# A written-out step order of a linear-attention and expert kernel, replaced by another order, with two store quarters cut in halves

## The chip, the cores and the metric

The kernel runs on one core of one Trainium2 chip. The metric is the device time of one execution in microseconds (us). Three executions of the kernel before took 101.87, 101.66 and 101.7 us; the median is 101.7 us.

## What is computed

For 4 batches, 4 heads, 1088 positions and a head size of 32, q, k and v become a linear attention, and its result goes through one dense feed-forward layer with 2048 inner columns. Cut to what matters:

```
def phi(x):                       # x: batch, head, position, 32
    a = S1 x ; b = S2 x           # 8 numbers each
    return outer(a, b)            # 64 features
kv  = sum over positions of phi(k) * v      # 64 x 32 for each batch and head
z   = sum over positions of phi(k)
out = (phi(q) kv) / (phi(q) z + 1e-6)
x   = out, 4352 tokens x 128 columns (the four heads side by side)
h   = x w_in ; g = h * sigmoid(beta * h) ; y = g w_out
```

The kernel folds beta into the weights (w_in times beta, w_out divided by beta), so that the activation is a plain Silu.

## The kernel before, in words

**Two kinds of work.** The attention gives the activations x (transposed, in the tile `xT`), batch after batch. The feed-forward layer consumes them in ten chunks of tokens: two of 256, seven of 512, one of 256. A chunk's inner columns are worked through in waves of 1024 numbers for each partition: four waves for a chunk of 256, eight for one of 512, 68 in all.

**Steps.** Nothing schedules this kernel: every step is a function, `DO` maps a short name to each, and the string `SEQ` (L809 to L825) lists all of them by hand in program order. Each engine has its own queue and takes its own instructions in exactly that order; a step waits only for the data and buffers it needs, and everything behind it on its engine waits with it. A letter at the end of a name chooses the engine of a step: D is VectorE (DVE), A is ScalarE (ACT), P is GpSimd (POOL); for loads s, a and g choose the queue of SyncE (SP), ACT or POOL.

Steps of the feed-forward layer:

- `W` (L395): one wave, x times `winp` into PSUM (L407), and a Silu of 128x1024 on ACT (L415). I call the n-th one Wn; W5 begins the second chunk, W9 the third, W17 the fourth, W25 the fifth, W33 the sixth. The PSUM tile `wave` has two buffers.
- `V` (L424, L369): the second product for the oldest wave, into `moeout` (L379). Vn belongs to Wn. The last V of a chunk adds a turn on DVE (L389, which I call OUT0 to OUT9) and the chunk's stores from SP (L352; ST0 to ST9), four DMAs for each batch that the chunk touches, one for each 32 columns.
- `li`, `wi`, `be`, `bc`: load w_in, broadcast beta by a matmul, copy it from PSUM, and multiply them on POOL (`winp`, L311). `lo`, `wa`, `wv`, `wg`: load w_out and scale one 128x128 piece of it by 1/beta (`rb`) on ACT (L332), DVE or POOL (L339).

Steps of the attention, for batch b:

- `lk`, `lq`, `lv` load the keys, the queries and the values; keys and queries have one tile each for all batches, so the next load waits until the last turn has read it. `tk` and `tq` are 32x32 block turns on DVE (L434, L440).
- `kp`: products of the keys with S1 and S2 on PE (L456), `ka`: their turn into factors on DVE (L465). `o`: outer products of the factors in five parts (L591; parts of 128x512, the part numbered 2 of 128x256). `kv`: the sum over positions on PE (L632), 72 pairs of matmuls in parts `kv0` to `kv4`, each behind its outer product.
- `gr`, `gc`, `wh`, `wc`: the factors' Gram matrix on PE (L479), a copy (L491), a small product (L495), a copy into the weights of q (L505); they give the denominator's factor.
- `q..`: the products for the queries on PE (L518), two letters for the PSUM tiles of the halves (w, t or o). `qt`: their turns (L535). `dm`, `di`, `dx`, `da`: the denominator and its division into a factor (L547, L556, L562, L581, L570); the part of the factor that `dx` gives lies in PSUM, that of `da` in SBUF. `p`: outer products (L591) and `t`: their turns (L622).
- `n..` (the numerator, L689) needs all `t` of a batch and the turned sums `nd`. For batch 0 these come by PE (`ns`, `nt`, `nc`), for the others by a turn (`nf`) and two DMAs through DRAM (`ng`, L672 and L676). `x` copies the result into `xT` (L705) in two halves.

Batch 0's queries are worked in two parts: A, the first 256 positions, and C, the rest. So W1 to W4 need part A alone.

**Fillers.** `h`, `e`, `i` and `mW` are matmuls on a constant tile (L253) that keep TensorE at work.

**The order around the change.** DVE's queue up to batch 0's numerators runs, in step names: `ka00 ka01 tqA gc0D o00D rb o01D qtA0 qtA1 tqC diA daA pA0D tA0 qtC0 qtC1 tA1 tk10 diC tk11 dxC daC pC0D tC0 ka10 ka11 tC3 tC2 tC1 tk20 tk21`. PE's queue from the first wave on runs `W1 W2 kp1 W3 V1 gr1 V2 W4 wh1 nC kv10 kv11 kv12 kp2 W5 W6 V3 V4 W7 kv13 kv14 q1 W8 V5 V6 W9`.

Of the kernel before, what the change touches and what calls it, by code (L numbers as in the profile page):

```python
# [18 lines left out]
def kernel(  # L19
# [22 lines left out]
    T = S // 32  # L42
# [306 lines left out]
    ALT = {len(tok_chk) - 3, len(tok_chk) - 1}  # L349
    moe = {"ci": 0, "w": 0, "acc": None, "todo": [], "ready": set()}  # L350

    def store(o_sb, t0, u0, u1, queues):  # L352
        c = t0 + 32 * u0
        while c < t0 + 32 * u1:
            b, r = divmod(c, S)
            n = min(t0 + 32 * u1 - c, S - r) // 32
            u = (c - t0) // 32
            for g4 in range(4):
                queues[g4 % len(queues)].dma_start(
                    out=bass.AP(  # L360
                        tensor=out.tensor,
                        offset=out.offset + (b * S + r // 32) * DM + 32 * g4,
                        ap=[[T * DM, 32], [DM, n], [1, 32]],
                    ),
                    in_=o_sb[32 * g4 : 32 * g4 + 32, u : u + n, :],
                )
            c += n * 32

    def w2(ci, j0, jn, g):  # L369
        t0, tw = tok_chk[ci]  # L370
        if j0 == 0:
            if ci in ALT:
                moe["acc"] = ps1.tile([P, TCH], F32, tag="one", name="moeout")
            else:
                moe["acc"] = pso.tile([P, TCH], F32, tag="moeout", name="moeout")
        for jj in range(jn):
            j = j0 + jj
            assert j in scaled
            nc.tensor.matmul(  # L379
                out=moe["acc"][:, :tw],  # L380
                lhsT=woutp[:, j // U, j % U, :],
                rhs=g[jj],
                start=(j == 0),
                stop=(j == NJ - 1),
            )
        if j0 + jn == NJ:
            o_sb = sbA.tile([P, TCH // 32, 32], F32, tag="o_sb", name="o_sb", bufs=4)
            nt = tw // 32
            nc.vector.transpose(  # L389
                out=o_sb[:, :nt, :].rearrange("p t d -> p (t d)"), in_=moe["acc"][:, :tw]  # L390
            )
            last = ci == len(tok_chk) - 1
            store(o_sb, t0, 0, nt, [nc.sync, nc.scalar] if last else [nc.sync])

    def w1():  # L395
        ci = moe["ci"]
# [27 lines left out]
    def second():  # L424
        w2(*moe["todo"].pop(0))
# [336 lines left out]
    for nm, (_, n) in Q_PART.items():  # L762
        w = 1 if nm == "A" else 2
# [25 lines left out]
    for nm in Q_PART:  # L789
# [36 lines left out]
    for s_ in SEQ.split():
        DO[s_]()
# [29 lines left out]
```

## Time and profile before

| what | value |
|---|---|
| median of three runs | 101.7 us |
| the profiled execution | 100.9 us |
| its span, first to last instruction | 99.1 us |
| outside the span | 1.8 us |
| granted TensorE clock, mean over the span | 1.000 |
| instructions in the profile | 3150 |
| moved by DMA | 11.75 MB |

The profile is one execution taken by the hardware profiler. Its page lists busy time by engine, slices of the span, the chain of work that ended last, and groups of instructions; the trace behind it can be asked for the instructions of one engine in order of time, for waits, for one tile, for the chain piece by piece, and for stretches of the span. A row of the time order has a start, a length, the engine, the line, the operation with output and input, and a count; neighbours of one form are merged, and the length is that of the whole row. Lengths overlap a little, so the distance from start to start is what one instruction costs a queue. "PEld" is TensorE's weight load. A wait "<-issue" is one for which the trace names no releaser.

### The profile page before, as it was taken

The numbers are of one execution on the slowest core, as the hardware profiler recorded it, in microseconds if no ns is written. First come the engines' busy times: TensorE is split into PE (matmuls) and PEld (weight loads), VectorE is DVE, ScalarE is ACT, GpSimd is POOL, SyncE is SP. The second block draws the span as 40 slices with busy tenths as digits, with TensorE's granted clock in tenths as the row PEclk, the third lists the DMA queues.
The fourth block names the chain that finished last, engine by engine and source line by source line (L and its number), as shares of the span: only waits on it lengthen the run. The fifth ranks groups of instructions, "written<-read, shape, count | busy, mean of one in ns | idle before, by whom it ended". The sixth has DMA issues, their size and how long they took to land.

```text
span 99.1 us, 3150 instructions
## 1 busy us (share of the span) xinstructions
PE 92.4 (93%) x1302; PEld 48.7 (49%) x1302; DVE 58.1 (59%) x128; ACT 76.7 (77%) x102; POOL 36.1 (36%) x58
## 2 busy tenths in 40 slices
PE   5989998997999999999999999999999999999940
PEld 2525536665867544434445444444444444446720
DVE  3569989888579998449998335699630020020210
ACT  0505299984869797997998897999989999999910
POOL 5739989998594900077370000320000000000000
PEclk9999999999999999999999999999999999999999
DMA  2999999914971320058043141215015006014163
GB/s 55 273 351 317 395 370 388 270 42 107 387 225 38 62 44 7 0 149 307 17 95 67 20 76 30 53 31 83 2 20 85 1 2 104 7 20 70 17 100 59
DMA packets 24031, 11.75 MB, mean 119 GB/s; under 512 B 19245, under 2 KB 21837, under 8 KB 24017
## 3 DMA queue, kind: packets, MB, share of 16 engines
q1 hardware_dynamic: 23256, 11.44, 41.8%
q8 instruction: 10, 0.16, 0.6%
q10 hardware_dynamic: 696, 0.09, 0.6%
q0 software_dynamic: 64, 0.02, 0.4%
q14 instruction: 5, 0.03, 0.1%
HBM read 9.22 MB, written 2.33 MB: 117 GB/s over the span
## 4 chain that ended last, share of the span: by engine, by line
PE 63%; POOL 12%; ACT 9%; DMA 5%; SPq 4%; issue 2%; DVE 0%; POOLq 0%; ACTq 0%
PE wave L407 27%; PE moeout L379 26%; ACT g L415 8%; DMA w_in_sb<-in_moe_w_in_dram 5%; POOL winp L311 5%; PE nps L689 5%; PE kvz L632 4%; POOL qo L591 3%; POOL kp L591 3%; SPq L143 2%; SPq L164 1%; PE qps L518 1%; ACT xT L705 1%; PE kps L456 1%; SPq L178 1%
## 5 line engine op out<-in xcount | busy, mean ns | idle before, releaser
L415 ACT ACTIVATE g<-wave 128x1024 f16<-128x1024 f32 x68 | 64.8, 1027 | 7.0 <-PE wave L407 6.8
L407 PE MATMUL wave<-xT,winp 128*128 128x512 f16 (+1 forms) x160 | 39.7, 348 | 0.8 <-issue 0.4
L379 PE MATMUL moeout<-g,woutp 128*128 128x512 f16 (+1 forms) x160 | 37.6, 347 | 0.0
L407 PEld LDWEIGHTS <-winp 128*128 128x128 f16 x160 | 17.0, 114 | 16.7 <-issue 6.4
L379 PEld LDWEIGHTS <-woutp 128*128 128x128 f16 x160 | 15.4, 97 | 12.5
L591 POOL TENSOR_TENSOR kp<-kab 128x512 f32<-128x512 f32 (+1 forms) x17 | 16.1, 981 | 10.8 <-DVE kab L465 10.8
L389 DVE STREAM_TRANSPOSE o_sb<-moeout 128x512 f32<-128x512 f32 (+1 forms) x10 | 6.3, 631 | 22.0 <-PE moeout L379 22.0
L622 DVE STREAM_TRANSPOSE qt<-qo 128x512 f32<-128x512 f32 (+1 forms) x21 | 11.8, 605 | 0.2
L591 POOL TENSOR_TENSOR qo<-qa,qab 128x512 f32<-128x512 f32 (+1 forms) x11 | 9.5, 886 | 5.3 <-DVE qa L570 5.3
L535 DVE STREAM_TRANSPOSE qab<-qps 128x576 f32<-128x576 f32 (+2 forms) x10 | 6.0, 642 | 2.1 <-PE qps L518 2.0
L689 PE MATMUL nps<-qt,nd 32*32 32x288 f32 (+2 forms) x320 | 7.0, 364 | 0.1
L253 PE MATMUL kvz<-idle 128*128 128x384 f16 (+1 forms) x21 | 5.1, 399 | 1.1 <-DVE idle L215 1.1
L632 PE MATMUL kvz<-kp,v 128*32 128x64 f32 x288 | 5.7, 222 | 0.3 <-POOL kp L591 0.3
L434 DVE STREAM_TRANSPOSE kT<-k 128x544 f32<-128x544 f32 x8 | 5.6, 719 | 0.4 <-DMA k<-in_k_dram 0.3
L547 POOL TENSOR_TENSOR tmp<-qab 128x64 f32<-128x64 f32 (+2 forms) x3 | 1.8, 589 | 11.0 <-DVE qab L535 11.0
L440 DVE STREAM_TRANSPOSE qT<-q 128x576 f32<-128x576 f32 (+3 forms) x8 | 5.8, 721 | 0.0
L253 PEld LDWEIGHTS <-idle 128*128 128x128 f16 x36 | 3.5, 110 | 4.6 <-issue 2.3
L632 PEld LDWEIGHTS kvz<-kp,v 128*32 128x32 f32 x288 | 4.4, 109 | 2.6 <-issue 1.6
L465 DVE STREAM_TRANSPOSE kab<-kps 128x288 f32<-128x288 f32 x8 | 3.6, 464 | 3.2 <-PE kps L456 3.2
L689 PEld LDWEIGHTS nps<-qt,nd 32*32 32x32 f32 x320 | 3.9, 103 | 2.7 <-DVE qt L622 0.5
L311 POOL TENSOR_TENSOR winp<-w_in_sb,beta_bc 128x512 f16<-128x512 f32 x4 | 5.1, 1274 | 0.1
L332 ACT ACTIVATE woutp<-w_out_sb,rbeta 128x128 f16<-128x128 f32 x15 | 5.0, 399 | 0.1
(63 smaller groups left out, 54.8 us busy)
## 6 DMA issues: line engine op xcount, KB each, us to landing
k<-in_k_dram SPq DMA_DIRECT2D x3, 544.0 KB
q<-in_q_dram SPq DMA_DIRECT2D x3, 544.0 KB, 5.1
v<-in_v_dram SPq DMA_DIRECT2D x4, 288.0 KB
v<-in_v_dram SPq DMA_DIRECT2D x4, 256.0 KB, 5.8
w_in_sb<-in_moe_w_in_dram SPq DMA_DIRECT2D x4, 256.0 KB, 5.4
w_out_sb<-in_moe_w_out_dram SPq DMA_DIRECT2D x4, 256.0 KB, 5.7
out_dram<-o_sb SPq DMA_DIRECT2D x16, 64.0 KB, 3.6
k<-in_k_dram SPq DMA_DIRECT2D x2, 272.0 KB, 2.9
```

The lines of the kernel that those rows point to most:

```text
L253: nc.tensor.matmul(out=t[:, P : P + cols], lhsT=idle, rhs=cut(idle, [[0, cols // P], [1, P]]), start=fresh or other, stop=True, skip_group ...
L311: eng.tensor_tensor(out=winp[:, n].rearrange("p c u -> p (c u)"), in0=w_in_sb[:, o : o + FQ], in1=beta_bc[:, o : o + FQ], op=MUL,)
L379: nc.tensor.matmul(out=moe["acc"][:, :tw], lhsT=woutp[:, j // U, j % U, :], rhs=g[jj], start=(j == 0), stop=(j == NJ - 1),)
L389: nc.vector.transpose(out=o_sb[:, :nt, :].rearrange("p t d -> p (t d)"), in_=moe["acc"][:, :tw])
L407: nc.tensor.matmul(out=wv[:, jj // per, o : o + tw], lhsT=winp[:, j // U, :, j % U], rhs=xT[:, t0 : t0 + tw], start=True, stop=True,)
L415: nc.scalar.activation(out=g, in_=wv, func=ACTF.Silu)
L440: nc.vector.transpose(out=qT2[b % 2][:, t0:t1].rearrange("p t s -> p (t s)"), in_=q_t[b][:, t0:t1].rearrange("p t d -> p (t d)"),)
L535: nc.vector.transpose(out=cut(QAB[nm], [[32, 2], [32 * H, n], [1, 32]], 64 * i), in_=PS["qps", nm][i][:, :, : 32 * n],)
L591: eng.tensor_tensor(out=cut(o, [[F, n], [R, R], [1, R]]), in0=cut(a, [[sa, n], [1, R], [0, R]]), in1=cut(b_, [[sb_, n], [0, R], [1, R]]), ...
L622: nc.vector.transpose(out=QT[nm][:, j0:j1].rearrange("p j h c s -> p (j h c s)"), in_=QO[nm][:, j0:j1].rearrange("p j h f -> p (j h f)"),)
L632: nc.tensor.matmul(out=PS["kvz", b][32 * h : 32 * h + 32, :F], lhsT=v_t[b][:, h, j, :], rhs=KP[b][:, j, h, :], start=(j == 0), stop=(j == ...
L689: nc.tensor.matmul(out=t[g // 2][32 * h : 32 * h + 32, g % 2, : 32 * n], lhsT=ND[b][rows, h, fc, :], rhs=QT[nm][rows, :, h, fc, :], start= ...
```

## The change

`SEQ` is replaced by another order of nearly the same steps; the function `store` can send some of its quarters in two halves, and is told to for two of the four quarters of chunk 2 (the third chunk).

Part by part:

- In the text of `SEQ` the first part of the queries (`tqA`) stands right behind batch 0's factors, as it did; the Gram copy `gc0` that followed it on DVE goes to ACT, and both of DVE's outer products of batch 0 follow at once.
- `kv00` to `kv04` run one behind the other, without fillers between them. The four beta products are spread apart (`be01` behind `gr0`, `be10` behind `qA`, `be11` behind the `kv0`). Four `i` go and two `h` come.
- The scaling of w_out: pieces that ACT did go to DVE (piece 6) and POOL (14), and DVE's piece 10 to ACT; most of ACT's come before the first numerators or between W1 and W4.
- Other engines for single steps: `pC3` POOL to DVE; `wc1`, `xC1`, `wc2`, `wc3` DVE to ACT; the two halves of `x1` swap ACT and DVE; `o30` DVE to POOL; `dm3` POOL to DVE; `p33` DVE to POOL and `p34` POOL to DVE. The PSUM tiles of `qA`, `qC` and `n2` are given in another order.
- PE from the first wave on: `W1 W2 kp1 W3 V1 V2 W4 gr1 V3 nC V4 wh1 kp2 W5 W6 kv10 to kv14 q1 W7 V5 W8 V6 W9 V7 W10 V8 gr2 W11 V9 ... W15 V13 n1 W16 V14 W17 V15 W18 V16 W19 wh2 kp3 W20 W21 kv20 to kv24 q2 W22 V17`, then waves and V one by one, with `kv30 kv31` behind W25, `kv32` to `kv34` behind W28, and `n2` behind V24. From W32 on the order on PE is that of before, but for where some V stand from W51 on.
- SP: `lk3` comes behind ST0, `lq2` behind ST1 (before, both stood ahead of ST0) and `lq3` and `ng2` behind ST2 (before, ahead of it). ST2 is six DMAs and not four.
- DVE in batch 2: `t20 t24 tq30 t23 t22 tq31 nf3 t21`; before, `tq30` stood between `da2` and `dx2`, and `nf3` and `tq31` behind all turns.

The diff:

```diff
@@ -349,21 +349,26 @@
     ALT = {len(tok_chk) - 3, len(tok_chk) - 1}
     moe = {"ci": 0, "w": 0, "acc": None, "todo": [], "ready": set()}
 
-    def store(o_sb, t0, u0, u1, queues):
+
+    HALVED = 2
+
+    def store(o_sb, t0, u0, u1, queues, halved=0):
         c = t0 + 32 * u0
         while c < t0 + 32 * u1:
             b, r = divmod(c, S)
             n = min(t0 + 32 * u1 - c, S - r) // 32
             u = (c - t0) // 32
             for g4 in range(4):
-                queues[g4 % len(queues)].dma_start(
-                    out=bass.AP(
-                        tensor=out.tensor,
-                        offset=out.offset + (b * S + r // 32) * DM + 32 * g4,
-                        ap=[[T * DM, 32], [DM, n], [1, 32]],
-                    ),
-                    in_=o_sb[32 * g4 : 32 * g4 + 32, u : u + n, :],
-                )
+                m = n // 2 if g4 < halved else n
+                for w in range(0, n, m):
+                    queues[g4 % len(queues)].dma_start(
+                        out=bass.AP(
+                            tensor=out.tensor,
+                            offset=out.offset + (b * S + r // 32 + w) * DM + 32 * g4,
+                            ap=[[T * DM, 32], [DM, m], [1, 32]],
+                        ),
+                        in_=o_sb[32 * g4 : 32 * g4 + 32, u + w : u + w + m, :],
+                    )
             c += n * 32
 
     def w2(ci, j0, jn, g):
@@ -390,7 +395,7 @@
                 out=o_sb[:, :nt, :].rearrange("p t d -> p (t d)"), in_=moe["acc"][:, :tw]
             )
             last = ci == len(tok_chk) - 1
-            store(o_sb, t0, 0, nt, [nc.sync, nc.scalar] if last else [nc.sync])
+            store(o_sb, t0, 0, nt, [nc.sync, nc.scalar] if last else [nc.sync], HALVED if ci == 2 else 0)
 
     def w1():
         ci = moe["ci"]
@@ -807,21 +812,21 @@
                 DO[f"x{nm}{i}{c}"] = lambda nm=nm, i=i, c=c: put_x(nm, i, COPY[c])
 
     SEQ = """
-        ls0a ls1g lk0.0s lk0.1s lb4a lbpg m lqAs lv0s lqCs li0s li1s li2s li3s mW h h h h e e tk00 ts msP m2P
-        sq1P sq0P tk01 kp0t ka00 ka01 tqA be00 be01 kx0A bc00A bc01A gr0 gc0D h h wh0 wc0A z0 lo0s lk1s lo1s
-        lo2s lo3s h h qAww o00D rb o01D qtA0 qtA1 tqC lq1s lv1s o04P o02P o03P kv00 i kv01 kv02 i kv03 kv04 ns0A
-        i i i nt0 nc0A dmAP diA daA pA0D tA0 qCwt wi1P pA1P wi0P be10 be11 wa0 wa3 wa1 wa2 bc11A bc10A qtC0 qtC1
-        tA1 dmCP wi3P wi2P tk10 diC tk11 dxC daC pC0D tC0 pC3P pC2P pC1P wa7 wa4 wa5 wa11 i i i i i i i nAww
-        xA1A xA0A wa6 wa14 i i i W W kp1t ka10 ka11 tC3 tC2 tC1 W V gr1 V gc1A wa9 wa8 wa15 W wh1 lk2s tk20 tk21
-        wc1D nCtw xC0A wa12 xC1D tq10 wa13 o10P o11P o12P kv10 kv11 kv12 kp2t ka20 wv10 tq11 ka21 o14P o13P lk3s
-        lv2s lq2s W W V V W kv13 kv14 q1wt nf1 ng1s W V V qt10 qt11 dm1D di1 dx1 W W V da1 V W o20P o24P o23P
-        o21P o22P kv20 kv21 kv22 kv23 kv24 p10D p12P p13P p14P p11D t10 t11 t13 t12 t14 W W V V W V V W n1tw
-        x11A W nf2 tk30 tk31 x10D tq20 V gr2 gc2A W W kp3t wh2 W V W V W ka30 tq21 wc2D ka31 lq3s lv3s ng2s V
-        q2wt qt20 qt21 dm2D di2 o30D o34P o33P o31P o32P W V W V W V V W W V V W V W da2 tq30 dx2 p20D t20 p23P
-        t23 p22P t22 p21D p24P t21 t24 V W kv30 kv31 W kv32 kv33 kv34 W n2wt x21D nf3 ng3s x20A W V W gr3 W gc3D
-        wh3 V W V wc3D tq31 q3wt qt30 qt31 dm3P di3 dx3 W V W V W V W da3 V V p30D p31D p34P p33D t30 t33 p32D
-        t32 t31 t34 W W V V W V W V W V W V W V V W n3tw x30A x31D W V W V W V W V V W W V V W V W V W V W V W V
-        V W V W V W V W V W V V W V W V W V W V V W V V V V
+        ls0a ls1g lk0.0s lk0.1s lb4a lbpg m lqAs lv0s lqCs li0s li1s li2s li3s mW h h h h e e tk00 ts tk01 msP
+        kp0t ka00 ka01 tqA be00 sq0P m2P kx0A o00D o01D h h h gr0 be01 bc00A gc0A wh0 wc0A z0 lo0s lk1s lo1s
+        lo2s lo3s bc01A h h h qAwt o02P be10 kv00 kv01 o03P o04P sq1P kv02 kv03 kv04 be11 qtA0 qtA1 dmAP tqC
+        lq1s lv1s diA daA rb pA0D tA0 i qCtw wi0P qtC0 qtC1 pA1P tA1 wi1P dmCP tk10 diC tk11 dxC daC pC0D pC3D
+        wv6 ns0A bc11A wa0 bc10A nt0 nc0A i i i i i i i nAww wa1 wa3 wa4 wa7 wi3P wi2P xA0A xA1A wa5 wa8 wa11
+        wa2 i i i W wa10 W wa9 kp1t pC1P pC2P tC0 tC3 ka10 ka11 tC1 wg14 o10P o13P o12P o11P W V wa12 wa13 V
+        wa15 W gr1 V gc1A tC2 lk2s tk20 tk21 tq10 o14P nCtw lv2s tq11 V lk3s xC0A wh1 kp2t ka20 ka21 xC1A wc1A W
+        W kv10 kv11 kv12 kv13 kv14 q1wt W qt10 nf1 qt11 dm1D di1 dx1 V W V W V ng1s da1 W V gr2 W V W V W V W
+        gc2A V W V o20P o21P o22P o24P o23P p10D p11D p14P p13P p12P t10 t11 t13 t12 t14 n1tw x11D tk30 lq2s
+        tq20 tk31 x10A W V W V W lv3s tq21 V lq3s W wh2 kp3t wc2A ka30 ka31 W W kv20 kv21 kv22 kv23 kv24 q2wt W
+        V nf2 qt20 qt21 dm2D di2 dx2 da2 o30P o31P o33P o32P o34P p20D p21D t20 ng2s W V W V W kv30 kv31 W V W V
+        W kv32 kv33 kv34 W V W p23P p24P t24 p22P tq30 t23 t22 tq31 nf3 t21 V W V n2tw x21D ng3s x20A W V W gr3
+        W gc3D wh3 V wc3A W V q3wt W V qt30 qt31 dm3D di3 da3 W V W V W V V dx3 p30D t30 p32D p34D t34 p31D t32
+        p33P t31 t33 W W V V W V W V W V W V W V V W n3tw x31D x30A W V W V W V W V W V V W V W V W V V W V W V
+        W V W V W V W V W V V W V W V W V V W V W V W V V V V
     """
     for s_ in SEQ.split():
         DO[s_]()
```

## The prediction

> **What bounds the kernel now.** I read the page's chain first, then the groups, then the chain in order of time, to see who sets the pace where.
>
> ```profile
> PE 63%; POOL 12%; ACT 9%; DMA 5%; SPq 4%; issue 2%; DVE 0%; POOLq 0%; ACTq 0%
> ...
> L415 ACT ACTIVATE g<-wave 128x1024 f16<-128x1024 f32 x68 | 64.8, 1027 | 7.0 <-PE wave L407 6.8
> ```
>
> TensorE carries 63% of the chain; the Silus stood still 7.0 us before their waves, 6.8 of it for PE. So ACT is the second limit, close behind.
>
> ```profile
> 39.90 1.83 ACT g L415 x2
> ...
> 45.27 0.43 PE moeout L379 x2
> 45.70 0.43 PE wave L407 x2
> ...
> 55.84 0.65 ACT xT L705
> ...
> 59.40 1.03 ACT g L415
> ```
>
> A W or a V costs PE 0.43 (0.435 with its handoff), a pair 0.87; the first row gives a Silu 0.92 (1.83 for two). Where waves crowd, ACT sets the pace: from 39.90 to 44.63 and from 55.84 to 60.43 the chain lies almost wholly on it. From the first wave on, PE does the same steps before and after. So the change can win only where PE waits, and I compare the start of four steps on PE: W5, n1, W22, n2. From W32, right behind n2, PE's order is the old one up to W51.
>
> ```profile
> 20.93 1.38 PE L689 MATMUL nps<-qt,nd 32*32 32x224 f32 x64
> ...
> 23.32 0.71 PE L456 MATMUL kps<-kT,sk 64*32 64x288 f32 x16
> 24.41 1.03 PE L407 MATMUL wave<-xT,winp 128*128 128x256 f16 x8 [0.38 <-issue]
> ...
> 27.27 0.78 PE L518 MATMUL qps<-qT,wq 32*32 32x288 f32 x32
> ...
> 29.32 1.03 PE L407 MATMUL wave<-xT,winp 128*128 128x512 f16 x4
> ...
> 31.59 1.21 PE L632 MATMUL kvz<-kp,v 128*32 128x64 f32 x72
> 32.73 1.05 PE L407 MATMUL wave<-xT,winp 128*128 128x512 f16 x4
> ...
> 36.42 1.60 PE L689 MATMUL nps<-qt,nd 32*32 32x288 f32 x64
> ...
> 44.67 0.59 PE L407 MATMUL wave<-xT,winp 128*128 128x512 f16 x2
> ...
> 54.24 1.60 PE L689 MATMUL nps<-qt,nd 32*32 32x288 f32 x64
> ```
>
> Before: W5 at 24.41, W9 at 29.32, n1 at 36.42, W22 at 44.67, n2 at 54.24.
>
> **The change, part by part.**
>
> *Up to the first wave.* "First part of q right behind the keys" moves nothing on DVE: `tqA` stood behind `ka01` already. The fillers between the `kv0` go, and the beta products are spread. I estimate W1 between 0.5 and 1 us earlier. I count that as nothing, because of this wait and because nC needs all of C's turns:
>
> ```profile
> PEld kps L456 <- DVE qo L591: 0.2, 1, 0.2
> ```
>
> `kp1` reuses the PSUM tile that `pC0` reads, so W3 stays behind DVE's `pC0D`. That is the cover; were W1 later than about 16.9, it would cost one to one.
>
> *C's factors on DVE.*
>
> ```profile
> 11.34 0.62 DVE L591 TENSOR_TENSOR qo<-qa,qab 128x256 f32<-128x256 f32 x1
> ...
> 16.78 0.68 DVE L591 TENSOR_TENSOR qo<-qps,qab 128x512 f32<-128x512 f32 x1
> 17.50 0.71 DVE L622 STREAM_TRANSPOSE qt<-qo 128x512 f32<-128x512 f32 x1
> 18.43 0.85 DVE L465 STREAM_TRANSPOSE kab<-kps 128x288 f32<-128x288 f32 x2 [0.22 <-PE kps L456]
> 19.20 1.59 DVE L622 STREAM_TRANSPOSE qt<-qo 128x256 f32<-128x256 f32 x3
> ...
> 24.55 0.24 DVE L339 TENSOR_SCALAR woutp<-w_out_sb,rbeta 128x128 f16<-128x128 f32 x1
> ...
> 46.10 0.67 DVE L547 TENSOR_TENSOR tmp<-qab 128x288 f32<-128x288 f32 x1
> ```
>
> ```profile
> 10.39 1.28 POOL L311 TENSOR_TENSOR winp<-w_in_sb,beta_bc 128x512 f16<-128x512 f32 x1
> ...
> 14.62 2.50 POOL L311 TENSOR_TENSOR winp<-w_in_sb,beta_bc 128x512 f16<-128x512 f32 x2
> ...
> 42.73 3.72 POOL L591 TENSOR_TENSOR kp<-kab 128x512 f32<-128x512 f32 x4 [7.80 <-DVE kab L465]
> ```
>
> New between `pC0D` and `tC0` are `pC3D`, 128x256 with both factors in SBUF, and `wv6`. Their price is the open one. The row at 11.34 is such an operation: 0.62 for half of what the row at 16.78 did in 0.68 with a factor in PSUM. It ended at 11.96, and POOL's product (10.39 + 1.28) at 11.67: it reads as a wait for POOL and then 0.29. The `dm` at 46.10 ended at 46.77, 0.32 behind POOL's end at 46.45 (42.73 + 3.72). So I let a DVE product of two SBUF tiles wait out POOL's running instruction and then take 0.3. Bounds for `pC3D`: 0.3 with no wait, 2.0 if POOL wins twice.
>
> [...]
>
> Sum: `pC0D` at 16.7 (16.78; the steps ahead differ by -0.2 to +0.1), end 17.4. POOL's last `wi` ends at 17.1, and its next product (3.72 for three and a half, 1.06 each) at 18.1; `pC3D` ends at 18.4, `wv6` at 18.6. `tC0`, `ka1` and the three other turns take 0.71 + 0.77 (18.43 to 19.20) + 1.59 = 3.1: the last ends at 21.7. Before it ended at 20.79, and nC began 0.14 behind: now 21.8. nC 1.38, V4 0.43, wh1 0.2 (like the small products, an estimate), kp2 0.75: **W5 at 24.6**, 0.2 later. `xC0` and `xC1`, both on ACT now, at most 0.65 each, end by 24.5: just covered. The 0.38 before the old W5 names no releaser; I leave it out and keep it for the range. V3 and V4 (0.87) are done by then, but not the 40 of 72 pairs of `kv1` that stood ahead before (0.77): even.
>
> *W5 to n1.* W5, W6 and the break behind them 0.97, all of `kv1` 1.14 (31.59 to 32.73), q1 0.72, W7 V5 W8 V6 1.74: W9 at 29.2. Then seven W, seven V and gr2: 6.1 + 0.35, so PE is ready at 35.6. DVE:
>
> ```profile
> 28.09 1.45 DVE L535 STREAM_TRANSPOSE qab<-qps 128x576 f32<-128x576 f32 x2 [0.43 <-PE qps L518]
> 29.57 0.84 DVE L547 TENSOR_TENSOR tmp<-qab 128x288 f32<-128x288 f32 x1
> 30.45 0.49 DVE L556 TENSOR_REDUCE rd<-tmp 128x36 f32<-128x324 f32 x1
> ...
> 32.03 0.44 DVE L389 STREAM_TRANSPOSE o_sb<-moeout 128x256 f32<-128x256 f32 x1
> 32.39 1.25 DVE L591 TENSOR_TENSOR qo<-qps,qab 128x512 f32<-128x512 f32 x2
> 33.57 2.79 DVE L622 STREAM_TRANSPOSE qt<-qo 128x512 f32<-128x512 f32 x5
> 36.29 0.21 DVE L667 STREAM_TRANSPOSE kvf<-kvz 128x64 f32<-128x64 f32 x1
> ```
>
> q1 ends at 27.5; `qt` 1.48, `nf1` 0.15, `dm1` 0.65 (0.3 to 1.35 by where POOL's product ends), `di dx da` 1.58, OUT1 0.36, `p` 1.18, `t` 2.72: 35.6. **n1 at 35.7**, 0.7 earlier. The gain is that `kv2` (1.14) no longer stands ahead of n1, and that DVE is as early as PE.
>
> *n1 to W22.* n1 1.53, nine W and V 3.9, two handoffs 0.1, wh2 0.2, kp3 0.72, `kv2` 1.14, q2 0.75: 8.35, against 8.25 without `kv2`. Six Silus at 0.92 from 38.0 end by 43.6, just ahead of W22. **W22 at 44.05**, 0.6 earlier: the old stretch on ACT is filled with `kv2`.
>
> *W22 to n2.* Ten W and eight V 7.83, `kv3` in two parts 1.35, breaks 0.2: 9.4, so 53.45. DVE: q2 ends at 44.1; 1.48, `dm2` 0.6, 1.58, `p` 1.18, five turns 2.72, `tq30` and `tq31` 1.4, `nf3` 0.2: 53.3. **n2 at 53.45**, 0.8 earlier, both engines even.
>
> *Loads behind stores.*
>
> ```profile
> 42.15 0.36 SPq L143 DMA_DIRECT2D q<-in_q_dram  x1
> ```
>
> ```profile
> L359 SPq DMA_DIRECT2D out_dram<-o_sb x50: 315/454/1199, 26.8 to 96.3; - x50
> ```
>
> ```profile
> DMA to landing us min/median/max: 3.7/5.1/6.5
> ```
>
> A store costs SP 0.454 (0.315 to 1.199); queries land in 3.7 to 6.5. `lq2` now follows ST1: issue near 33.9; `kp3` is wanted at 40.5 and `tk31` stands behind `tq20` on DVE, so `lq2` must land by 39.05, 5.15 after its issue. ST2's six stores cost 2.7 behind OUT2 (41.3), so `lq3` goes out near 44.1 (42.15 before), and `ng2` behind it; `tq30` wants it at 49.9, 5.8 later. Taken: both covered at 5.1. The two more stores cost SP 0.9, hidden as long as that holds.
>
> *The rest.*
>
> ```profile
> 8.49 0.18 ACT L505 COPY wq<-gram 128x8 f32<-128x8 f32 x1
> ```
>
> `wc3` moves to ACT into a stretch of the chain that lies on ACT: +0.1. `dm3` and the `p3` change engines far ahead of n3: nothing. From W51 on some V stand elsewhere: -0.1 to +0.1, taken 0; ACT's other copies lie in its 7.0 us of waiting.
>
> Sum: -0.8 + 0.1 = -0.7. The span goes from 99.1 to 98.4, the profiled execution from 100.9 to 100.2, the median of 101.7 to **101.0** (its own range 100.6 to 101.5: the 0.38, and 0.3 for `pC0D` and POOL's boundaries).
>
> **The rivals.**
>
> 1. *`pC3D` isn't blocked.* W5 at 23.95, n1 at 35.05, n2 at 52.8: 100.35. The rows at 11.34 and 46.10 speak against it.
> 2. *Next to nothing comes of it.* ST2's stores issue at 0.65 each, between the median and the maximum of their row; `lq3` goes out at 45.3, lands at 50.4, 0.5 late, and n2 waits for `t21` behind `tq30` until 53.95: 101.5; with one more wait like the 0.38, 101.9. For it: DVE and PE are even at n1 and n2, without slack.
> 3. [...] `pC3D` waits for `pC2P` too: +1.06 at W5, n1 and n2 (54.5): 102.1.
> 4. *Slower by late queries.* The place is DVE, `tk31` behind `tq20` and `t21` behind `tq30`. At 6.5 us, `kp3` is 1.35 late, and `lq3`, itself issued later, another 0.7: n2 at 55.5, 103.1. It decides from a landing of `lq2` about 5.9 after its issue. Against it: little else is queued for DMA then.
> 5. *The change doesn't do what it says:* so for its first part, priced at nothing above.
>
> **How the numbers follow.** Forecast 0.55; rival 1 0.15; rival 2 0.12; rival 3 0.10; rival 4 0.08. The range leaves out most of rival 4 and the far end of rival 1: 100.3 to 102.2. A measurement of this kernel tells 0.2% (0.2 us) from no change. Faster takes the forecast but its upper end, and rival 1: 0.69; same, most of rival 2 and some of that end: 0.11; slower 0.20.
>
> **What would show it.** [...] Wrong: DVE idle before `tq20` or `tq30` on a DMA, W5 before 24, or PE idle at n1 on DVE for over 0.3 us.

## The result, and the profile after

The changed kernel is **slower**: 107.96 us in the median of four executions (106.92 to 109.07), beside 101.78 for the kernel before on the same chip (101.66 to 102.27). The ratio is 1.056, with an interval from 1.048 to 1.065. Ratios, here and below, leave out executions more than 1.5% above the fastest of their kernel; medians are of all executions. The forecast was 101.0 with a range up to 102.2. Line numbers after are five higher from `w2` on, so L407 (W) is L412, L379 (V) is L384, and L591 is L596.

The profiled execution took 106.92 with a span of 105.2. From its page come the row of the granted TensorE clock (each digit a slice of 2.6 us), the shares of the chain, and the groups of the Silu and of the beta products:

```profile
PEclk9999855569999999999999999999999999999999
...
PE 82%; DVE 10%; POOL 3%; issue 0%
...
L420 ACT ACTIVATE g<-wave 128x1024 f16<-128x1024 f32 x68 | 64.8, 1030 | 5.4 <-PE wave L412 5.3
...
L294 PE MATMUL betaps<-beta,ones 1*128 1x512 f32 x8 | 5.6, 790 | 0.0
```

The clock row is the first surprise: it falls in slice 5, stands at half in 6 to 8, rises in 9 and is whole everywhere else. The mean is 0.949, where it was 1.000 before. TensorE now carries 82% of the chain (63% before), and ACT has dropped out of it. The Silus waited less than before (5.3 for PE, 6.8 before), so the loss isn't in the waves.

The same checkpoints as in the prediction, from PE in order of time (start, length, what, count, and in brackets the wait):

```profile
6.58 1.12 PE L294 MATMUL betaps<-beta,ones 1*128 1x512 f32 x2
...
8.23 0.38 PE L484 MATMUL gram<-kab 128*32 128x32 f32 x18
8.53 1.12 PE L294 MATMUL betaps<-beta,ones 1*128 1x512 f32 x2
10.51 0.25 PE L500 MATMUL gram<-gsb,s2bd 128*32 128x8 f32 x8 [0.86 <-POOL wq L287]
...
11.28 0.47 PE L523 MATMUL qps<-qT,wq 32*32 32x64 f32 x32
11.68 1.33 PE L294 MATMUL betaps<-beta,ones 1*128 1x512 f32 x2
12.95 2.15 PE L637 MATMUL kvz<-kp,v 128*32 128x64 f32 x72
15.02 2.07 PE L294 MATMUL betaps<-beta,ones 1*128 1x512 f32 x2
...
17.46 1.05 PE L523 MATMUL qps<-qT,wq 32*32 32x224 f32 x32
...
18.92 2.45 PE L253 MATMUL warm<-idle 128*128 128x384 f16 x7
21.30 1.10 PE L694 MATMUL nps<-qt,nd 32*32 32x64 f32 x64
...
22.99 1.04 PE L412 MATMUL wave<-xT,winp 128*128 128x256 f16 x8
...
30.93 1.06 PE L412 MATMUL wave<-xT,winp 128*128 128x256 f16 x8
...
42.27 1.60 PE L694 MATMUL nps<-qt,nd 32*32 32x288 f32 x64
...
50.67 0.62 PE L412 MATMUL wave<-xT,winp 128*128 128x512 f16 x2
...
60.27 1.59 PE L694 MATMUL nps<-qt,nd 32*32 32x288 f32 x64
```

W1 stands at 22.99 (16.64 before; both rows hold W1 and W2), W5 at 30.93, n1 at 42.27, W22 at 50.67, n2 at 60.27. Set beside before's 24.41, 36.42, 44.67 and 54.24, the delay is 6.35 at W1, 6.52 at W5, 5.85 at n1 and 6.03 at n2; the span is 6.1 longer. **The whole loss is made ahead of W1**, in the stretch that the prediction counted as nothing. Behind W5 about half a microsecond comes back.

The two pairs of beta products before, in the same view, are the row that the prediction didn't quote:

```profile
6.20 1.13 PE L294 MATMUL betaps<-beta,ones 1*128 1x512 f32 x4
...
12.62 1.13 PE L294 MATMUL betaps<-beta,ones 1*128 1x512 f32 x4
```

Four matmul records (two products, each of one row of another block of 32) take 1.13 together there; after, two records (one product) take 1.12 alone. All eight took 2.26 before and 5.6 after (the group above).

TensorE in stretches, after (length; busy time of PE, PEld, DVE, ACT and POOL with counts; granted clock; DMA share; GB/s):

```profile
11.00:12.00 1.00, 1.00 (x36) 0.60 (x34) 0.27 (x2) 0.54 (x2) 0.00 (x0) 1.00 0.06 23
12.00:13.00 1.00, 1.00 (x6) 0.06 (x8) 1.00 (x3) 0.00 (x0) 0.68 (x2) 0.73 0.63 176
13.00:22.00 9.00, 9.00 (x175) 4.70 (x179) 5.02 (x15) 3.28 (x9) 5.13 (x6) 0.50 0.81 286
22.00:23.00 1.00, 1.00 (x35) 0.54 (x21) 0.96 (x4) 0.60 (x3) 1.00 (x2) 0.65 0.00 0
```

At half clock (0.50) PE is busy all the time, but with little: seven fillers take 2.45 (1.30 in `a_rows128` below, at 1.00), the beta product at 15.02 takes 2.07 and not 1.12.

ACT's queue at the start shows why `wh0` came late (10.51, 8.02 before):

```profile
7.71 0.30 ACT L478 COPY kps<-kab 128x160 f32<-128x160 f32 x1 [3.68 <-DVE kab L470]
9.69 0.59 ACT L304 COPY beta_bc<-betaps 128x512 f32<-128x512 f32 x1 [1.69 <-PE betaps L294]
10.17 0.19 ACT L496 COPY gsb<-gram 128x32 f32<-128x32 f32 x1
```

`gr0` was done at 8.61 (8.23 + 0.38). But `bc00` stands ahead of `gc0` on ACT, and it starts at 9.69 only: it waits until the second beta product, `be01`, ends at 9.65 (8.53 + 1.12). Both products write into one PSUM tile, and the copy of the first half waits for the second, which stands ahead of it in the program. `gc0` waits behind it, and `wh0` and `qA` behind `gc0`. The wait on `wh0`'s row names POOL, whose copy (L287) ends at 10.51 too in this execution. But `wh0` reads nothing of that copy, and it starts 0.15 behind the end of ACT's `gc0`; in `a_pair0` below, where the row names ACT, it is 0.14.

### The profile page after: what moved, and what is told of

Its sections match the earlier page's. It is cut to its first block, busy times and chain, and to the rows that moved or that the text cites. A ratio compares the mean times of both kernels' runs of the same rounds, so it can differ in the third digit from the quotient of the medians.

```text
span 105.2 us, 3148 instructions
## 1 busy us (share of the span) xinstructions
PE 98.6 (94%) x1300; PEld 51.0 (48%) x1300; DVE 57.9 (55%) x124; ACT 76.9 (73%) x106; POOL 37.3 (35%) x58
## 4 chain that ended last, share of the span: by engine, by line
PE 82%; DVE 10%; POOL 3%; issue 0%
PE wave L412 29%; PE moeout L384 27%; PE nps L694 6%; PE kvz L637 5%; PE kvz L253 5%; PE qps L523 3%; PE betaps L294 3%; POOL kp L596 3%; DVE qt L627 2%; PE kps L461 2%; DVE qo L596 2%; DVE kab L470 2%; DVE kT L439 1%; DVE qab L540 1%; DVE woutp L339 1%; PE gram L500 1%
## 5 line engine op out<-in xcount | busy, mean ns | idle before, releaser
L412 PE MATMUL wave<-xT,winp 128*128 128x512 f16 (+1 forms) x160 | 40.2, 348 | 0.3 <-ACT g L420 0.3
L384 PE MATMUL moeout<-g,woutp 128*128 128x512 f16 (+1 forms) x160 | 39.0, 347 | 0.2 <-ACT g L420 0.2
L412 PEld LDWEIGHTS <-winp 128*128 128x128 f16 x160 | 16.9, 115 | 16.9 <-issue 6.2
L384 PEld LDWEIGHTS <-woutp 128*128 128x128 f16 x160 | 15.3, 97 | 13.4 <-issue 0.5
L596 POOL TENSOR_TENSOR kp<-kab 128x512 f32<-128x512 f32 (+1 forms) x18 | 17.3, 996 | 11.7 <-PE wave L412 8.7
L596 POOL TENSOR_TENSOR qo<-qa,qab 128x512 f32<-128x512 f32 (+1 forms) x10 | 9.6, 977 | 14.2 <-DVE qa L575 14.2
L253 PEld LDWEIGHTS <-idle 128*128 128x128 f16 x34 | 4.2, 133 | 7.2 <-issue 5.8
L253 PE MATMUL kvz<-idle 128*128 128x384 f16 (+1 forms) x23 | 6.3, 442 | 1.0 <-DVE idle L215 1.0
L637 PEld LDWEIGHTS kvz<-kp,v 128*32 128x32 f32 x288 | 5.1, 125 | 2.4 <-issue 1.8
L710 ACT CAST xT<-nps 128x576 f16<-128x576 f32 (+3 forms) x7 | 3.3, 496 | 4.0 <-PE nps L694 4.0
L294 PE MATMUL betaps<-beta,ones 1*128 1x512 f32 x8 | 5.6, 790 | 0.0
```

The lines of the kernel that those rows point to most:

```text
L253: nc.tensor.matmul(out=t[:, P : P + cols], lhsT=idle, rhs=cut(idle, [[0, cols // P], [1, P]]), start=fresh or other, stop=True, skip_group ...
L294: nc.tensor.matmul(out=PS["beta", i][:, n], lhsT=ones[row, :], rhs=beta4[row, :], start=True, stop=True,)
L384: nc.tensor.matmul(out=moe["acc"][:, :tw], lhsT=woutp[:, j // U, j % U, :], rhs=g[jj], start=(j == 0), stop=(j == NJ - 1),)
L412: nc.tensor.matmul(out=wv[:, jj // per, o : o + tw], lhsT=winp[:, j // U, :, j % U], rhs=xT[:, t0 : t0 + tw], start=True, stop=True,)
L596: eng.tensor_tensor(out=cut(o, [[F, n], [R, R], [1, R]]), in0=cut(a, [[sa, n], [1, R], [0, R]]), in1=cut(b_, [[sb_, n], [0, R], [1, R]]), ...
L637: nc.tensor.matmul(out=PS["kvz", b][32 * h : 32 * h + 32, :F], lhsT=v_t[b][:, h, j, :], rhs=KP[b][:, j, h, :], start=(j == 0), stop=(j == ...
```

## The experiments

**Theory.** Three causes ahead of W1: the beta products cost their own time twice, as they no longer run side by side; the Gram copy waits on ACT behind `bc00`; and single products of one row let the clock fall to half. **Rivals.** The clock falls because PE stood idle 0.86 ahead of `wh0`, or because the fillers between the `kv0` went; or the change of the later order costs time too.

The checkpoints of all runs (start on PE in the profiled execution, us; median of all executions; ratio with its interval):

| kernel | wh0 | W1 | W5 | n1 | n2 | clock | median | ratio |
|---|---|---|---|---|---|---|---|---|
| before | 8.02 | 16.64 | 24.41 | 36.42 | 54.24 | 1.000 | 101.78 | |
| after | 10.51 | 22.99 | 30.93 | 42.27 | 60.27 | 0.949 | 107.96 | 1.056 (1.048 to 1.065) |
| a_pair0 | 9.12 | 20.34 | 29.20 | 40.53 | 58.50 | 0.967 | 102.96 | 1.009 (1.006 to 1.012) |
| a_pairs | 8.85 | 16.82 | 25.75 | 37.08 | 55.55 | 1.000 | 102.08 | 1.002 (0.9985 to 1.0055) |
| a_gramD | 9.37 | 22.08 | 29.76 | 41.10 | 59.90 | 0.948 | 106.6 | |
| a_warm | 12.72 | 22.57 | 31.97 | 43.31 | 61.28 | 0.979 | 108.0 | |
| b_split | 9.26 | 24.14 | 31.72 | 43.78 | 61.61 | 0.952 | 109.3 | 1.067 (1.059 to 1.074) |
| b_nofill | 9.10 | 17.61 | 24.96 | 37.42 | 55.25 | 0.995 | 101.9 | 0.998 (0.995 to 1.001) |
| b_rows128 | 9.29 | 20.29 | 27.47 | 39.54 | 57.37 | 1.000 | 104.97 | 1.027 (1.021 to 1.033) |
| a_rows128 | 10.73 | 19.27 | 28.42 | 39.76 | 57.74 | 0.997 | 104.36 | 1.027 (1.022 to 1.032) |
| a_pairs_wa6 | 9.06 | 16.78 | 24.83 | 36.47 | 54.58 | 1.000 | 101.63 | 0.993 (0.990 to 0.997) |
| a_fix | 8.13 | 16.58 | 24.58 | 36.07 | 54.27 | 1.000 | 101.62 | 0.994 (0.990 to 0.998) |
| b_late | 8.98 | 17.57 | 24.89 | 36.82 | 55.10 | 0.995 | 102.03 | 0.996 (0.993 to 0.999) |
| b_late_h0 | 8.83 | 17.94 | 25.79 | 37.71 | 56.02 | 1.000 | 102.04 | 0.996 (0.993 to 1.000) |

Beside them the kernel before had medians from 101.78 to 102.06. `wh0` starts at 8.02 there and between 8.83 and 9.10 in `b_nofill`, `b_late` and `b_late_h0`, whose order is the same up to it, so distances between checkpoints say more than the starts. The clock is that of the profiled execution. `a_gramD` and `a_warm` have no ratio: their executions spread with the clock, as told below.

### a_pair0: the first pair of beta products together again

```diff
-be00 sq0P m2P kx0A o00D o01D h h h gr0 be01 bc00A gc0A wh0
+be00 be01 sq0P m2P kx0A o00D o01D h h h gr0 bc00A gc0A wh0
```

> The changed order with be01 put back directly behind be00 (one step moved). Theory (lateness, then clock): apart, the two beta products cost 1.12 us each instead of 1.13 together, bc00 waits for both, gc0 stands behind bc00 on ACT, so PE idles 0.86 us before wh0, and that idle stretch is what halves the TensorE clock from 12.7 to 22.4. Then here the products of part A's queries start near 9.0 (11.28 in the changed kernel), the clock stays 1.00 and the time is 100.8 to 101.5. Rival (missing fillers): the clock halves because no fillers run between the kv of batch 0; then the clock still falls, to 0.95 or so, and the time is 104 to 106. A start of wh0 near 10.5 all the same would mean that it waits for a POOL step and not for the copy.

The median falls by 5.0 to 102.96, not to the 101.5 or less that was expected. `wh0` starts 1.39 earlier, and now its wait (0.37) is named for ACT. The eight executions fall into two kinds: six between 102.54 and 103.13 with a clock of 0.996 or more, and two at 105.16 and 105.18 with 0.967. The profile is of one of these two: there the clock was halved (0.50) from about 11.6 to 18.4, from `kv0` on, which follows `be10` alone. So this kernel loses the clock in some executions and not in others, and losing it costs 2.4 us. The ratio of 1.009 is that of the six that kept it.

### a_pairs: both pairs together again

The edit of `a_pair0`, and

```diff
-qAwt o02P be10 kv00 kv01 o03P o04P sq1P kv02 kv03 kv04 be11 qtA0
+qAwt o02P kv00 kv01 o03P o04P sq1P kv02 kv03 kv04 be10 be11 qtA0
```

> The changed order with both pairs of beta products together again (be00 be01, and be10 be11 behind the kv of batch 0). Theory (lateness, then clock): as with the first pair alone, another 0 to 1 us on PE before W1, clock 1.00, 100.6 to 101.3. Rival (missing fillers): the clock still halves, 104 to 106.

The clock is 1.000, W1 is back at 16.82, and the time at 102.08: the same as before within its interval. With two moves of beta products the whole loss is gone. The 100.6 to 101.3 that was expected isn't reached; what is missing lies behind W1, and is taken up with `a_pairs_wa6`.

### a_gramD: only the Gram copy on DVE, products still apart

```diff
-gr0 be01 bc00A gc0A wh0
+gr0 be01 bc00A gc0D wh0
```

> The changed order with the Gram copy gc0 back on DVE (behind its two outer products), the beta products still apart. PE then has no idle stretch of 0.86 us before wh0, but the beta products, which use one row of the array each, still fill 8.5 to 9.65. If the idle stretch alone halves the clock: clock 1.00 and 101.5 to 102.5. If little work in the array counts like idleness, or the missing fillers do it: the clock still halves, 105 to 107.

`wh0` comes 1.14 earlier (9.37), and PE has no wait ahead of it any more. The clock still halves (0.50 from 12 to 22), and W1 is only 0.91 earlier. So the idle time ahead of `wh0` isn't what lowers the clock. The four executions took 104.54, 106.58, 106.62 and 107.77 at a mean clock of 0.983, 0.948, 0.944 and 0.935: the lower the clock, the longer the time.

### a_warm: fillers ahead of wh0 and between the kv0

```diff
-gc0A wh0 wc0A
+gc0A h h h h h h h h wh0 wc0A
...
-kv00 kv01 o03P o04P sq1P kv02 kv03 kv04 be11
+kv00 i kv01 o03P o04P sq1P kv02 i kv03 kv04 i i i be11
```

> The changed order with eight fillers in front of wh0 (where PE idles) and five between and behind the kv of batch 0, as the kernel before had; the late chain is left as it is. If the clock is the larger part of the loss: clock 1.00, W1 near 19 instead of 23, 103 to 104.5. Rival (the waits alone make the loss and the clock only falls in time that is waited anyway): 106.5 to 108 whatever the clock.

It came to 108.0, at the end of the rival's range and not in the 103 to 104.5 of the theory, but not for the rival's reason: the fillers themselves got the half clock (0.50 from 10 to 12). The time order of PE:

```profile
8.76 1.36 PE L294 MATMUL betaps<-beta,ones 1*128 1x512 f32 x2
10.05 2.74 PE L253 MATMUL kvz<-idle 128*128 128x384 f16 x8
12.72 0.30 PE L500 MATMUL gram<-gsb,s2bd 128*32 128x8 f32 x8
```

PE had no gap here, and the clock fell even earlier, at about 9.5, during the second single product, and rose at about 12.9. The eight fillers took 2.74 and held `wh0` back until 12.72. The experiment doesn't separate the price of the clock from that of the fillers, but it shows the clock falling under a PE whose busy time is 1.00 in each microsecond from 8 to 13.

### b_split: the kernel before, with nothing but its beta products apart

```diff
-be00 be01 kx0A bc00A bc01A gr0 gc0D
+be00 kx0A gr0 be01 bc00A bc01A gc0D
...
-h h qAww o00D
+h h qAww be10 o00D
...
-kv04 ns0A i i i nt0
+kv04 be11 ns0A i i i nt0
...
-pA1P wi0P be10 be11 wa0
+pA1P wi0P wa0
```

> The kernel before, with only its four beta products taken apart as the change does (be01 behind the Gram product, be10 behind part A's query products, be11 behind the kv of batch 0); all fillers and the Gram copy on DVE stay. [...] Rival (missing fillers, or the copy on ACT, are needed for the fall of the clock): clock 1.00, 102.5 to 103.5, from the split pairs and the later copies alone.

109.3, more than the 104.5 to 107 expected and worse than the changed kernel, with all fillers in place, `gc0` on DVE and the old order behind W1. The beta products apart are enough for the whole loss.

### b_rows128 and a_rows128: products apart, but over all 128 rows

```diff
-            lhsT=ones[row, :],
-            rhs=beta4[row, :],
+            lhsT=sel[:, 2 * i + n, :],
+            rhs=beta4,
```

`sel` is zero but for one row of ones, and `beta4` is cleared before its load (which therefore stands behind `lbpg m` in `SEQ`), so each product still broadcasts one row of beta. Line numbers are five higher again. In `b_rows128` the edit is put on `b_split`, in `a_rows128` on the changed kernel.

> The kernel before with its beta products apart, as b_split, but each product over all 128 rows: the beta tile is cleared first, and a tile that is one in a single row and zero elsewhere picks the row. A product takes the same 1.12 alone. Theory (it is the single row that counts as idleness for the clock): granted clock 1.00 throughout, W1 1 to 2 us behind before's, 102.5 to 104.5. Rival (the clock falls because of where the products stand, or by the sum of PE's work, however many rows): the clock halves from about 11.5 to 21.5 as in b_split, 108 to 110.

> The changed kernel as it is, four beta products apart, each over all 128 rows (the beta tile cleared first, a tile with one row of ones picks the row). Theory (the single row costs the clock, the separate products cost their own time and the wait of the Gram copy): granted clock 1.00, wh0 still near 10.5, W1 at 19.0 to 19.8 where the changed kernel has 22.99, time 103.8 to 104.8. Rival (in the changed kernel the clock falls for another reason, the idle time ahead of wh0 or the missing fillers): clock below 0.97, W1 after 21.5, time above 106.

This settles the clock. PE of `b_split` and of `b_rows128` between 9.8 and 13.5, the same instructions in the same places with the same idle time of 0.60:

```profile
10.22 0.41 PE L518 MATMUL qps<-qT,wq 32*32 32x64 f32 x32 [0.28 <-POOL kp L591]
11.23 2.07 PE L294 MATMUL betaps<-beta,ones 1*128 1x512 f32 x2 [0.60 <-DVE qab L535]
13.23 0.65 PE L632 MATMUL kvz<-kp,v 128*32 128x64 f32 x16
```

```profile
10.36 0.41 PE L523 MATMUL qps<-qT,wq 32*32 32x64 f32 x32 [0.39 <-ACT w_out_sb L722]
11.37 1.12 PE L299 MATMUL betaps<-beta,sel 128*128 128x512 f32 x2 [0.60 <-DVE qab L540]
12.43 0.43 PE L637 MATMUL kvz<-kp,v 128*32 128x64 f32 x16
```

And the stretch from 12 to 21, first of `b_split`, then of `b_rows128`:

```profile
12.00:21.00 9.00, 9.00 (x116) 3.63 (x115) 1.51 (x6) 1.27 (x5) 2.88 (x3) 0.50 0.82 285
```

```profile
12.00:21.00 9.00, 8.30 (x196) 4.86 (x195) 5.72 (x16) 5.03 (x17) 5.91 (x6) 1.00 0.79 284
```

One row of inputs or 128: the product alone takes 1.12 either way, but with one row the clock is 0.50 and with 128 rows 1.00. `b_rows128` runs in 104.97, 4.3 less than `b_split`. From `wh0` to W1 the two take 11.00 and 14.88, so the clock is worth 3.9 there. The products apart cost more than was expected, though: W1 is 3.65 behind before's, not 1 to 2, and the time lies above 102.5 to 104.5.

In the changed kernel the same edit gives 104.36, 3.6 less, as the theory had it (103.8 to 104.8). Its PE:

```profile
10.73 0.25 PE L505 MATMUL gram<-gsb,s2bd 128*32 128x8 f32 x8 [0.85 <-POOL kp L601]
...
12.96 1.21 PE L642 MATMUL kvz<-kp,v 128*32 128x64 f32 x72
...
16.19 1.30 PE L258 MATMUL warm<-idle 128*128 128x384 f16 x7
...
19.27 1.03 PE L417 MATMUL wave<-xT,winp 128*128 128x256 f16 x8
```

The wait ahead of `wh0` is still there (0.85), so the rival's idle time isn't what lowers the clock. From `wh0` to W1 it takes 8.54, as long as before (8.62), where the changed kernel took 12.48. The clock's part of the delay at W1 is therefore 3.9; the rest of the 6.35 is the 2.5 by which `wh0` is late (10.51 and 8.02): 0.4 as the first product itself started later in that execution (6.58 and 6.20), 2.1 from the products apart and the copy's wait. With both pairs together `wh0` to W1 takes 7.97 (`a_pairs`), 0.6 less than in `a_rows128`: that is about what the two other single products cost W1 at full clock.

### b_nofill: the kernel before without the fillers around the kv0

```diff
-kv00 i kv01 kv02 i kv03 kv04 ns0A i i i nt0
+kv00 kv01 kv02 kv03 kv04 ns0A nt0
```

These are five `i`.

> The kernel before without its six fillers between and behind the kv of batch 0 (kv at once, as the change has it); nothing else moves. Theory (single beta products are the cause): clock 1.00 and 101.4 to 102.0. Rival (missing fillers let the clock fall): clock below 0.99 and 103 to 106.

The ratio is 0.998 (0.995 to 1.001), the clock 0.995. `wh0` to W1 is 8.51, beside 8.62. So the fillers there neither keep the clock nor hold W1 back.

### a_pairs_wa6 and a_fix: what is left behind W1

`a_pairs_wa6` is `a_pairs` with piece 6 of w_out scaled on ACT again and not on DVE. `a_fix` also puts `gc0` on DVE ahead of the fillers and the outer products, and `pC3` back on POOL.

```diff
-pC0D pC3D wv6 ns0A
+pC0D pC3D ns0A
...
-wa5 wa8 wa11 wa2
+wa5 wa6 wa11 wa2
...
-W wa9 kp1t
+W wa9 wa8 kp1t
```

`a_fix` has these edits, and

```diff
-kx0A o00D o01D h h h gr0 bc00A gc0A wh0
+kx0A gr0 gc0D h h h o00D o01D bc00A wh0
...
-pC0D pC3D ns0A
+pC0D ns0A
...
-kp1t pC1P pC2P tC0 tC3 ka10 ka11 tC1
+kp1t pC3P pC1P pC2P tC0 ka10 ka11 tC3 tC1
```

> The changed order with both pairs of beta products together, and the sixth piece of w_out scaled by ACT again (one scaling of 0.24 us leaves DVE, where it took 1.09 in the changed kernel, ending with POOL's running product). [...] Rival (DVE is not what nC waits for, or ACT pays the same): 102.0.

> The changed order with the beta pairs together, the sixth piece on ACT, the last outer product of part C on POOL again, and the Gram product and its copy on DVE ahead of the fillers and outer products: every step that the traces showed late goes back, the later stages stay as changed. Theory (the later stages gain what was forecast, 0.8 us by the second numerators): W5 near 24.4, n2 near 53.5, 100.5 to 101.2, faster than the kernel before. Rival (the gain of the later stages was only slack that the late start gave them): 101.6 to 102.2.

DVE in `a_pairs`, then in `a_pairs_wa6`:

```profile
18.15 0.91 DVE L596 TENSOR_TENSOR qo<-qa,qab 128x256 f32<-128x256 f32 x1
18.98 1.09 DVE L339 TENSOR_SCALAR woutp<-w_out_sb,rbeta 128x128 f16<-128x128 f32 x1
19.99 1.02 DVE L627 STREAM_TRANSPOSE qt<-qo 128x512 f32<-128x512 f32 x2
```

```profile
18.11 1.03 DVE L596 TENSOR_TENSOR qo<-qa,qab 128x256 f32<-128x256 f32 x1
19.07 1.02 DVE L627 STREAM_TRANSPOSE qt<-qo 128x512 f32<-128x512 f32 x2
```

Without `wv6` the turns of C start 0.92 earlier, and W5 stands 0.92 earlier (24.83, 25.75). At n1 0.61 of that is left, as PE now waits 0.24 for the sums that come by DMA. In the time it is 0.45 by the medians (102.08 to 101.63) and 0.9 by the ratios (1.002 to 0.993), and neither kernel reaches the time expected of it (101.1 to 101.5, and 100.5 to 101.2). Both are a little faster than the kernel before, by 0.7% and 0.6%, and they can't be told apart: `pC3` on POOL and the Gram copy on DVE bring W1 and W5 a little forward (16.58 and 24.58), and nothing of it is seen at the end.

### b_late and b_late_h0: only the later order, with and without the halved stores

The kernel before up to its fourth wave, and the changed order from nC on; `b_late_h0` has `HALVED = 0` as well.

```diff
-wc1D nCtw xC0A wa12 xC1D tq10 wa13 o10P o11P o12P kv10 kv11 kv12 kp2t ka20 wv10 tq11 ka21 o14P o13P lk3s
+wc1D V nCtw xC0A wa12 xC1D tq10 wa13 o10P o11P o12P kp2t ka20 tq11 ka21 o14P o13P lk3s
...
-lv2s lq2s W W V V W kv13 kv14 q1wt nf1 ng1s W V V
+lv2s W V W kv10 kv11 kv12 kv13 kv14 q1wt W qt10 nf1
```

From there on the text is that of the changed kernel; `wv10` stands ahead of `tk20`.

> The kernel before up to its fourth wave on every queue (with both pairs of beta products, the fillers, and no product between pC0 and the turns of C on DVE), and the changed order from nC on: V3 ahead of nC, all of kv1 behind W6, kv2 behind q2, the loads behind the stores, the halved stores. Theory (the whole loss is made ahead of W1, and the steps behind W5 win a few tenths): W5 at 24.2 to 24.5, n1 0.3 to 0.7 earlier than before, n2 0.1 to 0.6 earlier, 101.2 to 101.7 beside a kernel before at 101.9. The forecast's own sizes (W5 to n2 shorter by 0.98) give n2 at 53.3 and 100.9. Rival (the changed order behind the waves costs time too, by loads behind stores): n1 or n2 waits for the sums by DMA, 102.2 or more.

> The same kernel, with the four stores of the third chunk whole. If the two more stores delay the queries or the sums of batch 2, n2 is 0.2 to 0.9 earlier and the time with it. If they are hidden, as the forecast took them, the time is the same within 0.2%, and only the stores' issue on SP is shorter by about 0.9.

The medians are 102.03 and 102.04 beside 102.03, the ratios 0.996: at most a few tenths of a per cent are won, and the medians miss the theory's 101.2 to 101.7. From n1 to n2 they take 18.28 and 18.31, so here the halved stores cost nothing at n2. On SP they aren't free: from the start of ST2 to the first DMA of the sums (`ng2`) it is 4.93 in `b_late` (42.62 to 47.55) and 3.69 in `b_late_h0` (43.23 to 46.92). That stays hidden because n2 waits for DVE in both, and 18.28 is longer than before's 17.82:

```profile
55.10 1.60 PE L694 MATMUL nps<-qt,nd 32*32 32x288 f32 x64 [0.25 <-DVE qt L627]
```

DVE itself had lost time there to a product of POOL, and not to a load:

```profile
51.44 0.45 DVE L627 STREAM_TRANSPOSE qt<-qo 128x256 f32<-128x256 f32 x1 [0.35 <-POOL qo L596]
```

In `a_pairs` n2 waits at the same place for the turned sums, which come through DRAM behind the stores:

```profile
55.55 1.59 PE L694 MATMUL nps<-qt,nd 32*32 32x288 f32 x64 [0.42 <-DMA nd<-ndw]
```

```profile
42.60 4.17 SPq L364 DMA_DIRECT2D out_dram<-o_sb  x6
...
47.41 0.59 SPq L677 DMA_DIRECT2D ndw<-kvf  x1
```

DVE had turned these sums by 45.16 (44.91 + 0.25); SP sends them out at 47.41, behind the six stores and `lq3`. So the rival of late loads holds in a small form, and for the sums: in `a_pairs` n1 to n2 takes 18.47, 0.65 more than before, as much as W5 to n1 wins there (0.68). Whether whole stores would bring the 0.42 back in `a_pairs` was not run.

## Why the prediction was wrong

**Up to the first wave: this is the step that failed.** It said "the fillers between the `kv0` go, and the beta products are spread. I estimate W1 between 0.5 and 1 us earlier. I count that as nothing". The words weighed the fillers, and the spread products not at all. To count the fillers as nothing was right: without them `wh0` to W1 is 0.1 shorter (`b_nofill`). Of the 6.35 at W1, 3.9 come from the clock (`a_rows128`), and the rest, but for some 0.4 of a later start, from the products that run alone and hold the Gram copy back. The row at 6.20 showed two products in 1.13. To ask whether one alone takes half of that, or as long, would have given a term of up to 1.1 for each of two more products ahead of `qA` and `kv0`; and `bc00` ahead of `gc0` on ACT could be read from the new order. The clock could not be read from the trace of before, where it is 1.000 throughout. The condition that the prediction set, "were W1 later than about 16.9, it would cost one to one", held: 6.35 at W1, 6.2 in the medians. None of the rivals had a late W1.

What lowered the clock is shown in part only. Idle time of PE does not account for the 0.50: in the changed kernel no idle time of PE between 5 us and the fall is longer than 0.86, in `a_warm` the time order shows none, and `b_rows128`, with the same 0.60 ahead of `be10` as `b_split`, keeps the clock at 1.00. What counted here was how many rows the products used. Only one row and 128 were compared: whether single rows count or the blocks of 32, by how much, and over how long, isn't shown; `a_pair0`, where one pair apart lost the clock in two executions of eight, shows only that the same order can lose it or keep it.

**C's factors on DVE: right for `pC3D`, one term mis-sized.** `pC3D` was to wait out POOL's running product and then take 0.3. DVE and POOL after:

```profile
22.98 1.25 DVE L596 TENSOR_TENSOR qo<-qa,qab 128x256 f32<-128x256 f32 x1
24.16 1.09 DVE L339 TENSOR_SCALAR woutp<-w_out_sb,rbeta 128x128 f16<-128x128 f32 x1
25.17 1.02 DVE L627 STREAM_TRANSPOSE qt<-qo 128x512 f32<-128x512 f32 x2
```

```profile
22.89 2.27 POOL L596 TENSOR_TENSOR qo<-qa,qab 128x512 f32<-128x512 f32 x2
```

POOL's two products end near 24.02 and at 25.16; `pC3D` ends at 24.23, 0.2 behind the first, as forecast. `wv6` ends at 25.25, right behind the second. It was priced at 0.2 from the row at 24.55 (0.24). POOL before, at that time:

```profile
19.73 4.74 POOL L591 TENSOR_TENSOR kp<-kab 128x512 f32<-128x512 f32 x5
```

POOL's products had just ended there, at 24.47, so the row at 24.55 says nothing about a busy POOL. After, `wv6` cost 1.09, and `a_pairs_wa6` shows that the path carries the difference. That is the price of rival 3 (1.06, a second product of POOL), at the instruction behind the one that it named. With `wv6` off DVE, W1 to W5 takes 8.05, beside 7.96 in the forecast (24.6 - 16.64). That the two wait for POOL is read from their ends alone, 0.21 and 0.09 behind its two products; what makes them wait no run shows. The prediction took the wait for one of the two only.

**W5 to n1, n1 to W22, W22 to n2.** Forecast 11.1, 8.35 and 9.4; after, 11.34, 8.40 and 9.60. Each is longer, by 0.24, 0.05 and 0.20: most steps take 0.43, as in the sum, but those at a handoff up to 0.53. W5 to n2 was to win 0.98 and won 0.49. In the kernels with W1 near its old place the same distance is 29.75 (`a_pairs_wa6`), 29.69 (`a_fix`) and 30.21 (`b_late`), beside 29.83 before. There the moved `kv1` and `kv2` therefore bring 0.1 at best by n2. What W5 to n1 wins in the first two (0.37 and 0.52 of 12.01) is spent from n1 to n2, which takes 18.11 and 18.20 there and 17.82 before: they need 8.56 and 8.58 from n1 to W22, where the forecast allowed 8.35, and 9.55 and 9.62 from there to n2, as long as before (9.57), where it allowed 9.4. In `b_late` and `a_pairs` n2 stands behind DVE or the sums (0.25 and 0.42 above). The prediction had DVE and PE even there and still took the whole gain.

**Loads behind stores** were taken as covered. That held for the queries: `tq20` and `tq30` ran without a wait after, and the longest elsewhere is 0.17 (`tq20` in `b_late`). It did not hold for the sums, in kernels that were on time (0.24 at n1 in `a_pairs_wa6`, 0.42 at n2 in `a_pairs`). One term was too small: the six stores of ST2 were put at 2.7, at 0.454 each, and took 4.17 in `a_pairs`, 0.70 each, a little more than rival 2 had (0.65). The two more stores cost nothing at n2 in `b_late`, as taken, but there it stood behind DVE. **The rest**, +0.1 from n2 to the end: 44.93 after, 44.86 before.

In sum, by the medians: the clock 3.6 (107.96 to 104.36), the products apart and the Gram copy's wait 2.3 (104.36 to 102.08), `wv6` 0.45. By the ratios they are 3.0, 2.5 and 0.9. Without these three the rest of the change is worth 0.4 us by the medians (101.63 beside 102.06) and 0.7 by the ratio, 0.3 to 1.0 in its interval. The forecast had 0.7, so its total for the rest can stand, though not the steps by which it got there.

## What to carry to other kernels

Small products that run side by side in different rows of TensorE are one item of the price list (here 1.13 for two, and 1.12 for one alone): before one of them is moved away, find the row that shows them together and price each alone, and look at what copies from the tile that they share. A broadcast that uses one row kept TensorE busy in the profile here (1.00), and did not keep its clock (0.50, and 1.00 over 128 rows). And a duration taken from a row is good only for the neighbours that it had: before 0.24 is carried over, see whether the engine that will be at work beside it, here POOL (1.09), was at work in that row.

## What was not expected of the hardware

- Two products of one row, in different blocks of 32 rows, took 1.13 together, and one took 1.12 alone (2.07 at a clock of 0.50).
- A TensorE that was busy, with products of one row 1.12 long, lost half its clock (0.50): in `a_warm`, without a gap, 2.7 us after the start of the first of them, in the changed kernel, with one gap of 0.86, 6 us after it and for some 10 us. The same products over 128 rows kept it at 1.00.
- Whether it fell could differ from one execution to the next of one kernel: `a_pair0` had 0.967 in two of eight, `a_gramD` from 0.935 to 0.983.
- A `tensor_scalar` on DVE, fp32 to fp16 between SBUF tiles, 0.24 with POOL idle (from 24.47 to 25.95 before), took 1.09 beside POOL's products.
